# First loads on two queues, masks in another order, one sink product for all heads, and the spread of the inverse sums after the second turn

## The chip, the cores and the metric

The kernel runs on one core of a Trainium2 chip. The metric is the device time of one execution in microseconds (us). Three executions of the kernel before took 599.73, 600.29 and 600.51 us; their median, 600.29 us, is the time before.

## The reference

Attention over 2 batches of 8 heads, 768 positions and 64 dimensions, in which a position sees the last 128 positions (`window`) and the first 4 (`n_sink`), both given as run-time numbers. Then two feed-forward layers of 512 to 2048 to 512, each with weights in 64-bit floats, on the 1536 token rows.

```python
keep = is_sink | in_window                      # pos < n_sink, or 0 <= rel < window
scores = np.where(keep, scale * q @ k.T, -1e9)
a = np.exp(scores - max); a = a / (a.sum() + 1e-09)
x = (a @ v) as rows of 512
h = x @ w_in;  x = (h * tanh(log1p(exp(h)))) @ w_out        # first layer
h = x @ w_in2; x = (h * clip(h + 3, 0, 6) / 6) @ w_out2     # second layer
```

## The kernel before, in words

The token rows are cut into twelve units of 128 positions (all 8 heads each), numbered 0 to 11; units 0 to 5 are batch 0. `BLOCKS` groups them: 6, 7, 0, 1, then 2, 3, 4, 5, then 8 to 11. The eight units of the first two groups are done at the very start, in float32, by class `First` (lines 309 to 422); the last four are done later in pieces beside the layers. The layers split float32 values into two float16 parts and take three products for each.

For each of the eight first units, `prep` (L315) transposes keys and queries on TensorE (L323) and copies them out on ScalarE (L326); `scores(g)` (L337), for a half g of the heads, multiplies (L350), adds the mask and takes the minimum on VectorE (L354) and exponentiates on ScalarE (L358); `turn(g)` (L363) transposes the weights (L369) and copies them out (L371 on ScalarE, L373 on VectorE); `values(g)` (L382) multiplies by v (L393) into the PSUM tile `o`. Units at place 2 or later in their batch (units 2 to 5) see sink positions that lie outside their two blocks. For them `turn(g)` also gathers 16 sink columns for each of 4 heads (L377), transposes that (L379) and copies it out as `ats` (L380), and `values(g)` begins with two products of `ats` with `vsb` (L388), a block matrix of the first 16 value rows, built once on GpSimd (L306).

`inverse` (L398) takes the inverse of the sums on VectorE (L401, L402), spreads it over 64 columns on GpSimd (`rb`, L405), transposes that on TensorE (L407) and copies it out on ScalarE (`rib`, L409). `normalise` (L411) multiplies `o` by `rib` (`xf`, L413) and `outputs` (L415) splits the result (L419, L420).

`first_blocks` (L424) emits the steps of the eight units in an interleaved order: turn(0) of a unit, scores(0) of the next, outputs of the unit before, values(0), prep of the unit after the next, inverse, turn(1), scores(1) of the next, values(1), normalise. A scheduler then orders each engine's instructions: it keeps to the order of emission as priorities, and moves work that is ready into gaps. The decoding of the 64-bit weights on VectorE and ScalarE (L210 to L224) lies in such gaps. `keep_in_program_order` pins an instruction to its place.

At the start SP's queue issues, in this order, the two parameters (L110), keys and queries of the first unit (6), keys and queries of the second (7), then values, the third unit, and the first weights. VectorE sets three constants and zeroes `warm` (L929), on which 12 matmuls run (L932). `emit_params` (L107) turns the two parameters into floats as soon as they land, `emit_masks` (L122) builds the identity that all transposes use (`ident`, L128), the masks `m0`, `m1`, `m2` and the selector `selh`.

Of the kernel before, what the change touches and what calls it, by code (L numbers as in the profile page):

```python
# [7 lines left out]
F32 = mybir.dt.float32  # L8
# [21 lines left out]
def attention_moe_moe2(  # L30
# [59 lines left out]
    selh = const.tile([128, 4], F32)  # L90
    ident = const.tile([128, 128], F32)
# [15 lines left out]
    def emit_params():  # L107
        raw = const.tile([128, 2, 2], I32)
        for i, a in enumerate((n_sink, window)):
            nc.sync.dma_start(out=raw[:, i, :], in_=a.bitcast(I32).rearrange("(o t) -> o t", o=1).to_broadcast([128, 2]))  # L110
        f = const.tile([128, 2, 2], F32)
        t = const.tile([128, 2, 2], F32)
        nc.vector.tensor_copy(out=f, in_=raw)
# [8 lines left out]
    def emit_masks():  # L122
        ns, wd = nsw[:, 0:1], nsw[:, 1:2]
        tmp = part_p.tile([128, 4, 128], F32, tag="part", name="tmp")
        col, rel, ind, dg = (tmp[:, i] for i in range(4))
        nc.gpsimd.iota(col, pattern=[[1, 128]], base=0, channel_multiplier=0, allow_small_or_imprecise_dtypes=True)
        nc.gpsimd.iota(rel, pattern=[[-1, 128]], base=0, channel_multiplier=1, allow_small_or_imprecise_dtypes=True)
        nc.vector.tensor_scalar(out=ident, in0=rel, scalar1=0.0, scalar2=None, op0=ALU.is_equal)  # L128

        nc.vector.tensor_scalar(out=ind, in0=rel, scalar1=0.0, scalar2=None, op0=ALU.is_ge)  # L130
        nc.vector.scalar_tensor_tensor(out=dg, in0=rel, scalar=wd, in1=ind, op0=ALU.is_lt, op1=ALU.mult)
        nc.vector.tensor_scalar(out=m2[:, 0:128], in0=dg, scalar1=-BIG, scalar2=BIG, op0=ALU.mult, op1=ALU.add)

        nc.vector.scalar_tensor_tensor(out=ind, in0=col, scalar=ns, in1=dg, op0=ALU.is_lt, op1=ALU.max)
        nc.vector.tensor_scalar(out=m0, in0=ind, scalar1=-BIG, scalar2=BIG, op0=ALU.mult, op1=ALU.add)

        nc.vector.tensor_scalar(out=ind[:, 0:16], in0=col[:, 0:16], scalar1=ns, scalar2=None, op0=ALU.is_lt)
        nc.vector.tensor_scalar(out=m2[:, 256:272], in0=ind[:, 0:16], scalar1=-BIG, scalar2=BIG, op0=ALU.mult, op1=ALU.add)
# [6 lines left out]
        hp = const.tile([128, 4], F32)  # L145
        nc.gpsimd.iota(hp, pattern=[[-16, 4]], base=0, channel_multiplier=1, allow_small_or_imprecise_dtypes=True)
        a = const.tile([128, 4], F32)
        b_ = const.tile([128, 4], F32)
        nc.vector.tensor_scalar(out=a, in0=hp, scalar1=0.0, scalar2=None, op0=ALU.is_ge)
        nc.vector.scalar_tensor_tensor(out=a, in0=hp, scalar=16.0, in1=a, op0=ALU.is_lt, op1=ALU.mult)  # L150
        nc.vector.tensor_scalar(out=b_, in0=hp, scalar1=64.0, scalar2=None, op0=ALU.is_ge)
        nc.vector.scalar_tensor_tensor(out=b_, in0=hp, scalar=80.0, in1=b_, op0=ALU.is_lt, op1=ALU.mult)
        nc.vector.tensor_tensor(out=selh, in0=a, in1=b_, op=ALU.add)
# [133 lines left out]
    def load_first(u, names="kqv"):  # L287
        b, i = divmod(u, NSB)
        rows = slice(i * 128, (i + 1) * 128)
        for nm, src, pool, tag in (("k", k, n_p, "n"), ("q", q, n_p, "n"), ("v", v, v_p, "v")):  # L290
            if nm in names:
                t = pool.tile([128, H, D], F32, tag=tag, name="first")
                nc.sync.dma_start(out=t, in_=src[b, :, rows, :].rearrange("h p d -> p h d"))
                qkv_n.setdefault(u, {})[nm] = t

    def first_sinks(b):


        ks1 = c_p.tile([128, HP, 16], F32, name=f"ks1_{b}")
        nc.scalar.activation(out=ks1, in_=kv_n[b * NSB][0][:, :, 0:16], func=AF.Copy)  # L300
        vsn = c_p.tile([64, 2, D], F32, name=f"vsn_{b}")
        for g in range(2):
            nc.sync.dma_start(out=vsn[:, g, :], in_=v[b, 4 * g:4 * g + 4, 0:16, :])
        vsb = c_p.tile([64, 2, 4, D], F32, name=f"vsb_{b}")
        for h in range(4):
            nc.gpsimd.tensor_scalar(out=vsb[:, :, h, :], in0=vsn, scalar1=selh[0:64, h:h + 1], scalar2=None, op0=ALU.mult)  # L306
        sink_n[b] = (ks1, vsb)

    class First:
        def __init__(self, u):  # L310
            self.u = u
            self.b, self.i = divmod(u, NSB)
            self.d, self.at, self.ats = [None, None], [None, None], [None, None]
# [23 lines left out]
        def scores(self, g):  # L337
# [5 lines left out]
            for h0 in (4 * g, 4 * g + 2):  # L343
# [7 lines left out]
                for r in range(2):  # L351
                    h = h0 + r
                    hh = h % 4
                    nc.vector.tensor_tensor_reduce(  # L354
                        out=d[:, hh, 0:n], in0=sps[r], in1=self.mask, scale=SCALE, scalar=BIG,
                        op0=ALU.add, op1=ALU.min, accum_out=self.mins[:, h:h + 1],
                    )
                    nc.scalar.activation(  # L358
# [4 lines left out]
        def turn(self, g):  # L363
# [10 lines left out]
            if self.i > 1:  # L374
                ats = self.ats[g] = s_p.tile([64, 128], F32, tag="ats", name="ats")
                ds = s_p.tile([128, 4, 16], F32, tag="ds", name="ds")
                nc.vector.tensor_copy(out=ds, in_=d[:, :, 256:272])  # L377
                tp = ps_acc.tile([64, 128], F32, tag="acc", name="tp")
                nc.tensor.transpose(tp, ds.rearrange("p h s -> p (h s)"), ident)  # L379
                nc.vector.tensor_copy(out=ats, in_=tp)  # L380

        def values(self, g):  # L382
            if g == 0:
                self.o = ps_h.tile([128, HP, 128], F32, tag="h", name="o")
            if self.i > 1:
                for c in (2 * g, 2 * g + 1):
                    vsb = sink_n[self.b][1][:, g, 2 * (c % 2):2 * (c % 2) + 2].rearrange("p h d -> p (h d)")
                    nc.tensor.matmul(self.o[:, c, :], vsb, self.ats[g], start=c == 0, stop=False, skip_group_check=True)  # L388
            for c in (2 * g, 2 * g + 1):
                for m, kv in enumerate(self.kvs):  # L390
                    for r in range(2):
                        h = 2 * c + r
                        nc.tensor.matmul(  # L393
                            self.o[64 * r:64 * r + 64, c, :], kv[1][:, h, :], self.at[g][:, m, h % 4, :],
                            start=self.i <= 1 and c == 0 and m == 0, stop=c == HP - 1 and m == len(self.kvs) - 1, skip_group_check=True,
                        )

        def inverse(self):  # L398
# [3 lines left out]
            nc.vector.reciprocal(out=ri[:, :, 0], in_=rs)  # L402
            tp = ps_acc.tile([128, HP, 128], F32, tag="acc", name="tp")
            rb = b_p.tile([128, H, D], F32, tag="rb", name="rb")
            nc.gpsimd.tensor_copy(out=rb, in_=ri.to_broadcast([128, H, D]))  # L405
# [18 lines left out]
    def first_blocks():  # L424
# [4 lines left out]
        us[0].scores(0)  # L429
        us[1].prep(True)  # L430
        us[0].scores(1)
        for n, e in enumerate(us):
# [14 lines left out]
            e.turn(1)  # L447
            if f:
# [462 lines left out]

    nc.scalar.preload_act_table_set("natural_log_exp_and_others")
    nc.vector.memset(one, 1.0)
    nc.vector.memset(fifth, 0.2)
    nc.vector.memset(bias3, 3.0)
    emit_params()
    load_first(first[0], "kq")
# [69 lines left out]

    nc.vector.tensor_scalar(out=bads[:, 0:1], in0=nsw[:, 0:1], scalar1=16.0, scalar2=None, op0=ALU.is_gt)
    nc.vector.tensor_scalar(out=bads[:, 1:2], in0=nsw[:, 1:2], scalar1=128.0, scalar2=None, op0=ALU.is_gt)
    nc.vector.scalar_tensor_tensor(out=bads[:, 1:2], in0=nsw[:, 1:2], scalar=1.0, in1=bads[:, 1:2], op0=ALU.is_lt, op1=ALU.max)  # L990
# [190 lines left out]
NWARM = 12  # L1181
# [40 lines left out]
```

## Time and profile before

| what | value |
|---|---|
| three executions, median | 600.29 us (599.73 to 600.51) |
| the profiled execution, its own time | 599.53 us |
| its span, first to last instruction | 597.7 us |
| TensorE busy | 579.0 us, 97% of the span |
| VectorE busy | 457.8 us, 77% |
| ScalarE busy | 398.4 us, 67% |
| GpSimd busy | 24.8 us, 4% |

The profile is of one execution. Engines are called PE (TensorE matmul), PEld (TensorE weight load), DVE (VectorE), ACT (ScalarE), POOL (GpSimd) and SP (the sync engine, whose queue SPq issues loads). A row of the timeline has the start in us, the duration in us, engine, line, operation, output and inputs, a count where rows were merged, and in square brackets the idle time of the engine before it with what ended it. The chain of waits follows the execution back from its last instruction, at each step to what released it. About the first 97 us hold the eight first units; the layers fill the rest.

### The profile page before, as it was taken

To read this page: it belongs to the slowest core of one execution; us is meant where nothing else is said; L and a number is where in the kernel's file an instruction comes from. 1 tells how busy PE (TensorE), PEld (TensorE's weight loads), DVE (VectorE), ACT (ScalarE), POOL (GpSimd) and SP (SyncE) were. 2 spreads that over 40 slices of the span, in tenths; PEclk is the share of its full clock that TensorE was granted. 3 is DMA by queue.
4 is the path that set the end of the run, shared out by engine and by line. 5 is a ranking of instruction groups with operands and counts; after the bars stand their busy time and mean duration, and the time that the engine had idled before them with its cause. 6 is when DMAs were issued, how large, how long until landed. Compare 5 with 4: busy or idle time off the path is not lost.

```text
span 597.7 us, 11394 instructions
## 1 busy us (share of the span) xinstructions
PE 579.0 (97%) x4430; PEld 394.4 (66%) x4430; DVE 457.8 (77%) x1102; ACT 398.4 (67%) x786; POOL 24.8 (4%) x36
## 2 busy tenths in 40 slices
PE   7999999999999999899989999999999999999996
PEld 4778754444444545444434468888888888888885
DVE  5688998999365555489999999866687889874754
ACT  5998887777687776679888887434354656553532
POOL 0040010700000000000000000000000000000000
PEclk9999999999999999999999999999999999999999
DMA  9976357998334533254453442000007676400001
GB/s 179 226 163 212 101 183 199 230 261 213 96 73 74 80 60 73 47 159 141 157 192 122 163 143 71 1 1 2 1 7 249 215 263 223 142 34 1 36 1 39
DMA packets 105842, 72.24 MB, mean 121 GB/s; under 512 B 73512, under 2 KB 98088, under 8 KB 105784
## 3 DMA queue, kind: packets, MB, share of 16 engines
q1 hardware_dynamic: 105784, 71.48, 42.9%
q8 instruction: 35, 0.57, 0.4%
q14 instruction: 23, 0.19, 0.1%
HBM read 60.43 MB, written 3.15 MB: 106 GB/s over the span
## 4 chain that ended last, share of the span: by engine, by line
PE 59%; DVE 13%; ACT 12%; issue 11%; DMA 2%; POOL 2%; SPq 1%; DVEq 0%; ACTq 0%
PE acc L846 18%; PE h L806 7%; PE h L808 7%; PE h L807 7%; PE acc L782 6%; PE h L737 3%; PE h L739 2%; PE h L738 2%; DVE p L212 2%; ACT e L745 2%; ACT e L746 2%; DVE g L754 2%; ACT d L358 2%; ACT y L215 1%; PE o L393 1%
## 5 line engine op out<-in xcount | busy, mean ns | idle before, releaser
L782 PE MATMUL acc<-g,w 128*128 128x512 f16 x576 | 131.2, 379 | 5.4 <-DVE g L754 5.1
L846 PE MATMUL acc<-w,g 128*128 128x256 f16 x1008 | 113.8, 273 | 0.0
L846 PEld LDWEIGHTS <-g 128*128 128x128 f16 x1008 | 98.6, 98 | 11.4
L806 PE MATMUL h<-xt,w 128*128 128x256 f16 x384 | 104.7, 273 | 0.0
L808 PE MATMUL h<-xt,w 128*128 128x256 f16 x384 | 104.7, 273 | 0.0
L807 PE MATMUL h<-xt,w 128*128 128x256 f16 x384 | 104.7, 273 | 0.0
L782 PEld LDWEIGHTS <-w 128*128 128x128 f16 x576 | 55.3, 98 | 71.6 <-issue 7.0
L737 PE MATMUL h<-xt,w 128*128 128x512 f16 x192 | 72.8, 379 | 1.8 <-DVE mins L558 1.2
L739 PE MATMUL h<-xt,w 128*128 128x512 f16 x192 | 72.8, 379 | 0.0
L738 PE MATMUL h<-xt,w 128*128 128x512 f16 x192 | 72.8, 379 | 0.0
L810 ACT ACTIVATE e<-h,bias 128x512 f32<-128x512 f32 x48 | 32.5, 678 | 54.5 <-PE h L808 54.5
L811 DVE SCALAR_TENSOR_TENSOR e<-e,h 128x512 f32<-128x512 f32 x48 | 32.8, 684 | 41.8 <-ACT e L810 41.8
L823 ACT ACTIVATE g<-e 128x256 f16<-128x256 f32 x96 | 29.5, 354 | 28.8 <-DVE e L811 28.8
L823 ACT ACTIVATE g<-sm 128x512 f16<-128x512 f32 x48 | 30.2, 628 | 27.5 <-DVE sm L818 27.5
L749 DVE SCALAR_TENSOR_TENSOR e<-e,h 128x512 f32<-128x512 f32 x48 | 30.8, 683 | 16.5 <-ACT e L747 16.3
L824 DVE SCALAR_TENSOR_TENSOR g<-sm,g 128x512 f16<-128x512 f32 x48 | 33.1, 689 | 10.9 <-ACT g L823 10.8
L806 PEld LDWEIGHTS <-w 128*128 128x128 f16 x384 | 37.6, 98 | 4.6
L807 PEld LDWEIGHTS <-w 128*128 128x128 f16 x384 | 37.6, 98 | 4.5
L808 PEld LDWEIGHTS <-w 128*128 128x128 f16 x384 | 37.6, 98 | 4.3
L212 DVE SCALAR_TENSOR_TENSOR p<-raw,y 128x1024 int32<-128x1024 int32 x32 | 39.8, 1243 | 0.4
L740 ACT ACTIVATE e<-h 128x512 f32<-128x512 f32 x48 | 28.1, 588 | 16.4 <-PE h L739 16.4
L754 DVE SCALAR_TENSOR_TENSOR g<-e,g 128x1024 f16<-128x1024 f32 x24 | 29.4, 1226 | 8.3 <-ACT g L753 8.3
(172 smaller groups left out, 934.8 us busy)
## 6 DMA issues: line engine op xcount, KB each, us to landing
raw<-in_moe_w_in_dram SPq DMA_DIRECT2D x48, 512.0 KB, 4.2
raw<-in_moe_w_out_dram SPq DMA_DIRECT2D x48, 512.0 KB, 5.0
out_dram<-ob SPq DMA_DIRECT2D x12, 256.0 KB, 2.5
first<-in_k_dram SPq DMA_DIRECT2D x8, 256.0 KB, 4.8
first<-in_q_dram SPq DMA_DIRECT2D x8, 256.0 KB, 4.9
first<-in_v_dram SPq DMA_DIRECT2D x8, 256.0 KB, 3.1
nk<-in_k_dram SPq DMA_DIRECT2D x5, 256.0 KB, 5.1
nv<-in_v_dram SPq DMA_DIRECT2D x5, 256.0 KB
```

What stands on the lines that cost most here:

```text
L212: nc.vector.scalar_tensor_tensor(out=p, in0=t[:, :, 1], scalar=3, in1=y, op0=ALU.logical_shift_left, op1=ALU.bitwise_xor)
L737: nc.tensor.matmul(o, wh, x[:, 0, c, :], start=c == 0, stop=False)
L738: nc.tensor.matmul(o, wh, x[:, 1, c, :], start=False, stop=False)
L739: nc.tensor.matmul(o, wl, x[:, 0, c, :], start=False, stop=c == KD - 1)
L754: nc.vector.scalar_tensor_tensor(out=gl, in0=e, scalar=sc, in1=gh, op0=ALU.mult, op1=ALU.subtract)
L782: nc.tensor.matmul(o, l_, r_, start=first and m == 0 and x == 0, stop=last and end and x == 2, skip_group_check=True)
L806: nc.tensor.matmul(o, wh, x[:, 0, c, :], start=c == 0, stop=False)
L807: nc.tensor.matmul(o, wh, x[:, 1, c, :], start=False, stop=False)
L808: nc.tensor.matmul(o, wl, x[:, 0, c, :], start=False, stop=c == KD - 1)
L823: nc.scalar.activation(out=g[:, 0, d_], in_=src, func=AF.Copy, scale=sc)
L824: nc.vector.scalar_tensor_tensor(out=g[:, 1, d_], in0=src, scalar=sc, in1=g[:, 0, d_], op0=ALU.mult, op1=ALU.subtract)
L846: nc.tensor.matmul(a[n // 2][:, n % 2], l_, r_, start=f == fa and m == 0 and n % 2 == 0 and x == 0, stop=ends and m == 1 and x == 2 and (n ...
```

## The change

It has these parts. At the start the parameters' loads are issued first, the first unit's keys go on ACT's queue and its queries on SP's; only then does ACT load its function table. On DVE `warm` is zeroed ahead of the three constants; `emit_fixed` builds `ident`, the causal indicator and the selectors before the parameters are converted; `emit_masks` builds only `m0`; the other masks and three range flags (`bads`, formerly emitted at the end) follow scores(0) of the first unit. Most of these are pinned to their order. There are 10 warm matmuls in place of 12.

For the sinks, `ds` gathers all 8 heads, one transpose and one copy of `ats` make 128 rows in place of 64 twice, `vsb` covers 128 rows with 8 GpSimd instructions in place of 4, its load is one DMA in place of two, and the sink products stand at the end of `values(1)` and no longer ahead of each half.

`inverse` keeps its DVE and POOL part; the four transposes of `rb` and the copy of `rib` move into `spread`, which is emitted after turn(1).

```diff
+    raw_p = load_params()
+    load_first(first[0], "k", nc.scalar)
+    load_first(first[0], "q")
     nc.scalar.preload_act_table_set("natural_log_exp_and_others")
-    emit_params()
-    load_first(first[0], "kq")
     load_first(first[1], "kq")
...
     nc.vector.memset(warm, 0.0)
+    nc.vector.memset(one, 1.0)
+    nc.vector.memset(fifth, 0.2)
+    nc.vector.memset(bias3, 3.0)
+    fixed = emit_fixed()
+    emit_params(raw_p)
...
-    emit_masks()
+    emit_masks(fixed)
...
-        us[0].scores(0)
+        us[0].scores(0, True)
+        emit_later_masks(fixed)
         us[1].prep(True)
...
             e.inverse()
             e.turn(1)
+            e.spread()
...
             if self.i > 1:
-                ats = self.ats[g] = s_p.tile([64, 128], F32, tag="ats", name="ats")
-                ds = s_p.tile([128, 4, 16], F32, tag="ds", name="ds")
-                nc.vector.tensor_copy(out=ds, in_=d[:, :, 256:272])
-                tp = ps_acc.tile([64, 128], F32, tag="acc", name="tp")
-                nc.tensor.transpose(tp, ds.rearrange("p h s -> p (h s)"), ident)
-                nc.vector.tensor_copy(out=ats, in_=tp)
+                if g == 0:
+                    self.ds = b_p.tile([128, H, 16], F32, tag="ds", name="ds")
+                nc.vector.tensor_copy(out=self.ds[:, 4 * g:4 * g + 4, :], in_=d[:, :, 256:272])
+                if g == 1:
+                    self.ats = b_p.tile([128, 128], F32, tag="ats", name="ats")
+                    tp = ps_acc.tile([128, 128], F32, tag="acc", name="tp")
+                    nc.tensor.transpose(tp, self.ds.rearrange("p h s -> p (h s)"), ident)
+                    nc.vector.tensor_copy(out=self.ats, in_=tp)
...
-            if self.i > 1:
-                for c in (2 * g, 2 * g + 1):
-                    vsb = sink_n[self.b][1][:, g, 2 * (c % 2):2 * (c % 2) + 2].rearrange("p h d -> p (h d)")
-                    nc.tensor.matmul(self.o[:, c, :], vsb, self.ats[g], start=c == 0, stop=False, skip_group_check=True)
...
+            if self.i > 1 and g == 1:
+                for c in range(HP):
+                    vsb = sink_n[self.b][1][:, 2 * c:2 * c + 2].rearrange("p h d -> p (h d)")
+                    nc.tensor.matmul(self.o[:, c, :], vsb, self.ats, start=False, stop=c == HP - 1, skip_group_check=True)
...
-NWARM = 12
+NWARM = 10
```

## Rows read from the trace of the kernel before

**Rows 1.** Busy us by stretch: length, PE, PEld, DVE, ACT, POOL, PEclk, DMA share, GB/s

```profile
9.00:20.00 11.00, 9.88 (x98) 7.88 (x100) 5.97 (x36) 10.92 (x41) 1.09 (x3) 1.00 1.24 259
20.00:30.00 10.00, 9.33 (x97) 7.07 (x94) 7.72 (x35) 8.89 (x29) 0.99 (x2) 1.00 0.75 192
...
40.00:50.00 10.00, 9.54 (x96) 7.99 (x97) 7.18 (x24) 8.88 (x25) 1.12 (x3) 1.00 0.59 190
...
60.00:72.00 12.00, 11.40 (x112) 9.33 (x112) 11.77 (x37) 9.89 (x28) 0.81 (x2) 1.00 0.28 89
72.00:97.00 25.00, 25.00 (x162) 13.93 (x162) 23.68 (x37) 19.71 (x29) 1.57 (x1) 1.00 0.63 191
97.00:150.00 53.00, 51.45 (x257) 23.18 (x256) 48.38 (x72) 40.52 (x57) 11.53 (x11) 1.00 0.89 226
```

**Rows 2.** Timeline of the first 10 us, all engines

```profile
0.80 1.28 ACT L912 ACT_TABLE_LOAD   x1 [0.80 <-PEq L1202]
...
1.35 4.30 PE L932 MATMUL wp<-warm 128*128 128x512 f16 x12 [1.35 <-DVE ones L998]
...
1.75 0.43 SPq L293 DMA_DIRECT2D first<-in_k_dram  x1
...
2.23 0.58 SPq L293 DMA_DIRECT2D first<-in_q_dram  x1
...
4.31 0.17 DVE L113 CAST f<-raw 128x4 f32<-128x4 int32 x1 [3.01 <-DMA raw<-in_window_dram]
...
6.34 1.09 PE L323 MATMUL tp<-ident,first 128*128 128x128 f32 x8 [0.69 <-DVE ident L128]
...
7.52 0.59 ACT L326 ACTIVATE qt<-tp 128x512 f32<-128x512 f32 x1
...
8.56 0.23 DVE L143 TENSOR_SCALAR m_all<-tmp 128x128 f32<-128x128 f32 x1
...
8.74 0.29 DVE L354 CUSTOM_DVE_ANT_0 d<-s,m 128x128 f32<-128x128 f32 x1
...
9.08 0.40 ACT L358 ACTIVATE d<-d,mins 128x128 f32<-128x128 f32 x1 [0.96 <-DVE mins L354]
```

**Rows 3.** DMA issues between 2.0 and 2.5 us: last number, us to landing

```profile
first<-in_q_dram SPq DMA_DIRECT2D x1, 256.0 KB, 4.4
```

**Rows 4.** Chain of waits, 15 to 88 us: start, us on the chain, what

```profile
15.23 0.44 PE tp L407 x4
...
24.43 0.60 PE tp L407 x4
...
59.14 1.07 POOL rb L405
60.25 0.67 PE tp L407 x4
60.94 0.60 ACT rib L409
...
87.40 0.59 PE tp L407 x4
```

**Rows 5.** Timeline of ACT, DVE, POOL and PE at `rib`, `xf` and the sinks

```profile
16.68 0.59 ACT L409 ACTIVATE rib<-tp 128x512 f32<-128x512 f32 x1
...
18.94 0.69 DVE L413 TENSOR_TENSOR xf<-o,rib 128x512 f32<-128x512 f32 x1 [0.49 <-PE o L393]
...
31.39 3.98 POOL L306 TENSOR_SCALAR vsb<-vsn,selh 64x128 f32<-64x128 f32 x4
...
46.24 0.71 PE L388 MATMUL o<-ats,vsb 64*128 64x128 f32 x4
...
49.57 0.60 ACT L409 ACTIVATE rib<-tp 128x512 f32<-128x512 f32 x1
...
54.07 0.69 DVE L413 TENSOR_TENSOR xf<-o,rib 128x512 f32<-128x512 f32 x1
```

**Rows 6.** Groups by line and shape up to 95 us: busy us, mean ns, idle before

```profile
L380 DVE COPY ats<-tp 64x128 f32<-64x128 f32 x8 | 2.2, 275 | 1.0 <-PE tp L379 1.0
```

More of the change, by code (lines that the diff above doesn't have):

```diff
@@ L90, in attention_moe_moe2 @@
     selh = const.tile([128, 4], F32)
+    sel8 = const.tile([128, H], F32)
     ident = const.tile([128, 128], F32)
@@ L120, in emit_params, with emit_fixed @@
         nc.vector.tensor_tensor(out=nsw, in0=t[:, :, 0], in1=t[:, :, 1], op=ALU.mult)
-    def emit_masks():
+    def emit_fixed():
+        tmp = part_p.tile([128, 4, 128], F32, tag="part", name="tmp")
+        col, rel, ind = (tmp[:, i] for i in range(3))
+        hp = const.tile([128, 4], F32)
+        nc.gpsimd.iota(rel, pattern=[[-1, 128]], base=0, channel_multiplier=1, allow_small_or_imprecise_dtypes=True)
+        nc.gpsimd.iota(col, pattern=[[1, 128]], base=0, channel_multiplier=0, allow_small_or_imprecise_dtypes=True)
+        nc.gpsimd.iota(hp, pattern=[[-16, 4]], base=0, channel_multiplier=1, allow_small_or_imprecise_dtypes=True)
+        keep_order(nc.vector.tensor_scalar(out=ident, in0=rel, scalar1=0.0, scalar2=None, op0=ALU.is_equal))
+        keep_order(nc.vector.tensor_scalar(out=ind, in0=rel, scalar1=0.0, scalar2=None, op0=ALU.is_ge))
+        a, b_ = (sel8[:, 0:4], sel8[:, 4:8])
+        keep_order(nc.vector.tensor_scalar(out=a, in0=hp, scalar1=0.0, scalar2=None, op0=ALU.is_ge))
+        keep_order(nc.vector.tensor_scalar(out=b_, in0=hp, scalar1=64.0, scalar2=None, op0=ALU.is_ge))
+        keep_order(nc.vector.scalar_tensor_tensor(out=a, in0=hp, scalar=16.0, in1=a, op0=ALU.is_lt, op1=ALU.mult))
+        keep_order(nc.vector.scalar_tensor_tensor(out=b_, in0=hp, scalar=80.0, in1=b_, op0=ALU.is_lt, op1=ALU.mult))
+        keep_order(nc.vector.tensor_tensor(out=selh, in0=a, in1=b_, op=ALU.add))
+        return tmp
@@ L123, in emit_masks @@
+    def emit_masks(tmp):
         ns, wd = nsw[:, 0:1], nsw[:, 1:2]
-        tmp = part_p.tile([128, 4, 128], F32, tag="part", name="tmp")
         col, rel, ind, dg = (tmp[:, i] for i in range(4))
-        nc.gpsimd.iota(col, pattern=[[1, 128]], base=0, channel_multiplier=0, allow_small_or_imprecise_dtypes=True)
-        nc.gpsimd.iota(rel, pattern=[[-1, 128]], base=0, channel_multiplier=1, allow_small_or_imprecise_dtypes=True)
-        nc.vector.tensor_scalar(out=ident, in0=rel, scalar1=0.0, scalar2=None, op0=ALU.is_equal)
@@ L140, in emit_masks, with emit_later_masks @@
+    def emit_later_masks(tmp):
+        ns, wd = nsw[:, 0:1], nsw[:, 1:2]
+        col, rel, ind, dg = (tmp[:, i] for i in range(4))
+        keep_order(nc.vector.tensor_scalar(out=m2[:, 0:128], in0=dg, scalar1=-BIG, scalar2=BIG, op0=ALU.mult, op1=ALU.add))
         nc.vector.tensor_scalar(out=dg, in0=rel, scalar1=128.0, scalar2=wd, op0=ALU.add, op1=ALU.is_lt)
@@ L292, in load_first @@
                 t = pool.tile([128, H, D], F32, tag=tag, name="first")
-                nc.sync.dma_start(out=t, in_=src[b, :, rows, :].rearrange("h p d -> p h d"))
+                ld = eng.dma_start(out=t, in_=src[b, :, rows, :].rearrange("h p d -> p h d"))
+                if pin:
+                    keep_order(ld)
                 qkv_n.setdefault(u, {})[nm] = t
@@ L300, in first_sinks @@
         nc.scalar.activation(out=ks1, in_=kv_n[b * NSB][0][:, :, 0:16], func=AF.Copy)
[L301 to L306, printed above, removed]
+        vsn = c_p.tile([128, D], F32, name=f"vsn_{b}")
+        nc.sync.dma_start(out=vsn, in_=v[b, :, 0:16, :])
+        vsb = c_p.tile([128, H, D], F32, name=f"vsb_{b}")
+        for h in range(H):
+            nc.gpsimd.tensor_scalar(out=vsb[:, h, :], in0=vsn, scalar1=sel8[:, h:h + 1], scalar2=None, op0=ALU.mult)
         sink_n[b] = (ks1, vsb)
@@ L312, in __init__ @@
             self.b, self.i = divmod(u, NSB)
-            self.d, self.at, self.ats = [None, None], [None, None], [None, None]
+            self.d, self.at = [None, None], [None, None]
         def prep(self, pin=False):
@@ L335, in prep, with scores @@
             self.mask = (m0, m1, m2)[min(i, 2)]
-        def scores(self, g):
+        def scores(self, g, pin=False):
             n = self.n
@@ L357, in scores @@
                     )
+                    if pin:
+                        keep_order(low)
                     nc.scalar.activation(
@@ L402, in inverse, with spread @@
             nc.vector.reciprocal(out=ri[:, :, 0], in_=rs)
+            self.rb = rb = b_p.tile([128, H, D], F32, tag="rb", name="rb")
+            nc.gpsimd.tensor_copy(out=rb, in_=ri.to_broadcast([128, H, D]))
+        def spread(self):
+            rb = self.rb
             tp = ps_acc.tile([128, HP, 128], F32, tag="acc", name="tp")
-            rb = b_p.tile([128, H, D], F32, tag="rb", name="rb")
-            nc.gpsimd.tensor_copy(out=rb, in_=ri.to_broadcast([128, H, D]))
             for c in range(HP):
```

44 lines of the change are left out of this document (17 added, 27 removed).

## The prediction

> **What bounds the kernel now.** I read the stretches first, then the timeline of the start, then the chain of waits. From 72 us on PE has work in nearly every microsecond: it is busy 25.00 of 25 us up to 97 and 51.45 of 53 up to 150 [rows 1]. Nothing in the change touches the layers, so what it can win lies in the first 97 us and shows as an earlier start of the layers. Those 97 us have several limits. Up to 9.08 us, when the first exponential runs, everyone waits for the start [rows 2]. From 9 to 20 us ACT is the limit, 10.92 busy of 11. From 20 to 30 and from 40 to 50 no engine is full: PE has 9.33 and 9.54 of 10, but its instructions overlap and that is latency, not work; DVE has 7.72 and 7.18, so 2.3 and 2.8 us in which DVE stands in the middle of a dependent chain. From 60 us on DVE is all but full: 11.77 of 12, 23.68 of 25, 48.38 of 53, because the decoding of weights fills its gaps [rows 1]. A shorter chain helps in full only where no engine is full.
>
> A measurement of this kernel can tell a difference of about 0.2%, 1.2 us, from no change; below 599.1 us counts as faster, above 601.5 as slower.
>
> **The start.** The queries are issued at 2.23 us and land 4.4 us later, at 6.63 [rows 2, 3]. The transposes stand at 6.34, after 0.69 us in which PE waited for `ident`, which is built behind the parameters although it doesn't need them; then come the copy of the queries at 7.52, the first mask operation at 8.74 and the exponential at 9.08. Two things arrive together at 8.74: the scores, and DVE itself, which builds `m1` until 8.79 (L143) before it turns to the scores [rows 2].
>
> Moving the keys to ACT's queue lets the queries take the SP place of the keys, 1.75 us, 0.48 us earlier. If the earlier keys (ACT is free at 0.80, some 0.9 us before 1.75) merely start the same stream of bytes earlier, the queries land 0.9 us earlier; if the second queue brings nothing, 0.48. With `ident` done before any key lands, the key transposes and their copy lie ahead of the queries, and the copy of the queries starts at landing + 0.55 (half of 1.09 for 8 transposes) + 0.1, so 7.28 by today's landing against 7.52: 0.24 us. Together 0.7 to 1.1 us. DVE's side keeps up: the parameters are converted at 4.31, seven operations of about that row's 0.17 us end at 5.5, and three mask operations, each as long as L143 (0.23) or half as long again, end `m0` near 6.5, where 7.7 is wanted; that is a cover of 1.2 us if the parameters land as now [rows 2]. The removed warm matmuls (2 of 12 in 4.30 us, 0.4 to 0.7 us of filler) lie in the 0.69 us PE idles before its first transpose: cost nothing. If PE ran its first transposes and scores at half rate for want of them, 1.09 us would double; that end I keep for the range. The later masks and range flags, ten DVE operations at the 0.23 us of L143, 2.3 us, move behind the first scores, where DVE waits for PE anyway; if they come in front of scores(1) they cost up to 0.5. The load that ACT now issues itself (0.43 us, as the same load takes on SP) pushes its table load of 1.28 us from 0.80 to 1.3; its first copy, of the keys, comes after 5 us [rows 2]. I take 1.0 us; ends 0 and 1.4. ACT is full from 9 to 20, so this shift is carried on whole as long as the loads keep ahead.
>
> The row that prices the second queue is the 4.4 us of one load among others [rows 3]; no row here has a load on ACT's queue. The Trainium skill, page "DMA: Bandwidth & Descriptors", section "Issuing engines are not separate DMA queues", says that loads started by different engines run on the same 16 DMA engines and interleave, so that only issue time is saved. By it the keys also stand in the way of the parameters; the start would win about 0.5 us, and the sum would be 2.7 in place of 3.2. The DMA share of 1.24 from 9 to 20 us [rows 1] agrees as far as it goes: the engines are the limit there, not the issuer.
>
> **The spread of the inverse sums.** Today PE has to run the four transposes of `rb` before the second turn, though turn(1) needs only exponentials that are done when POOL starts. At 59 us this is plain: POOL's 1.07 us, PE's 0.67 and ACT's 0.60 lie on the chain one behind the other. Ten such pieces, from 15.23 to 87.40 us, all others of 0.44 to 0.62, make 6.1 us [rows 4]. They are not removed, they go behind turn(1) and its copies, which the values wait for. At 15 and 87 us a full engine lies beside them, about 1.0 us that wins nothing. Of the 5.1 left, those at 24, 41 and 49 us (2.1 us) lie where DVE idles and count almost whole; those from 59 us on lie where DVE has under 1 us to spare [rows 1]. What is late next is the copy of the weights on ACT and the mask operations behind decoding. I take 1.6 us; ends 0 (another order of waits) and 5.1. `rib` itself comes about 1 to 1.5 us later. In the first unit it is done at 17.27 and wanted at 18.94, room of 1.7 us; in the fifth 50.17 and 54.07, room of 3.9 [rows 5].
>
> **The sinks.** Four units have them. For each, one of two transposes goes and one of two copies of `ats` on DVE (8 rows of 275 ns, some 0.2 us each where they overlap with the next [rows 6]). The products keep their count, four passes of 128 columns in 0.71 us for each half [rows 5]; on 128 rows they stream the same 128 columns, and I leave them at their price (ends: none, or a third of 8 x 0.71 = 5.7 us less). The first products no longer stand ahead of the values of half 0. DVE's 4 x 0.2 = 0.8 us counts, since DVE is full there; PE's transposes lie beside it. I take 0.6; ends 0 and 2.0. GpSimd's `vsb` becomes eight operations over half the columns: between 4 and 8 us in place of 3.98. It is built by 35.4 us and first read at 46.24, so 11 us hide it [rows 5]; at the upper end the next `rb` on POOL could be late by 2 us. One load fewer on SP, 0.6 us, hides too.
>
> **The sum.** 1.0 + 1.6 + 0.6 = 3.2 us. The profiled execution took 599.53 us (span 597.7 and 1.8 around it); 3.2 less is 596.3. The median lies 0.76 higher, so 597.1.
>
> **Rivals.** *DVE holds it.* From 60 to 150 us DVE is 91 to 98% busy, and what leaves the chain is refilled by the same decoding; PE then waits for DVE after 97 us, where today it idles only 1.55 us of 53 [rows 1]. Only DVE's own saving and part of the start come through: 0.8 + 0.4 = 1.2, so 599.3 (about no change). For it: those rows. Against: before 50 us DVE idles over 5 us in the two open stretches, and the decoding can be done earlier when everything is earlier. Chance 0.18.
>
> *Only issue time is saved at the start*, by the mechanism above: the keys and the queries share the 16 engines, and the tiny parameter loads share with them, so that `m0` comes as late as the scores. The start gives 0.5: 597.6. Chance 0.13, and faster all the same.
>
> *All that left the chain counts:* 1.2 + 4.0 + 1.3 = 6.5, so 593.8. The chain of waits lists these pieces one behind the other, which is for it; DVE's fill from 60 us is against. Chance 0.13.
>
> *`rib` becomes the last input of `xf`.* ACT copies it after the weights and, if the next unit's exponentials get in between (four of 0.40 us or longer [rows 2]), about 3 us later than now. Rooms are 1.7 to 3.9 us; the point from which it decides is about 2 us of delay. `xf` then holds the PSUM tile `o`, from the pool that the next scores use, and each of four units would lose 1.4 us (3.1 less 1.7): 5.6 lost, 2.6 won (start, spread partly, sinks), 3.0 slower: 603.3. Against it: `spread` is emitted ahead of scores(1) of the next unit, so its priority is higher. Chance 0.08.
>
> **Numbers.** My forecast has 0.48. Faster: 0.48 less a small tail of its own (0.02 to no change), and 0.13 and 0.13: 0.72. No change: 0.18 and that tail: 0.20. Slower: 0.08. The likeliest case gives 597.1, by itself 595 to 599. The range reaches down to 593.8, where all counts, and up to 600.3, where all three terms are at their lower ends: 593.8 to 600.3.
>
> **What would show it.** Right: the first exponential near 8.0 us in place of 9.08; first transposes no longer released by `ident` but by a load; no wait of PE for `rb`, and turn(1) ahead of the transposes of `rb` in every unit; four copies of `ats` in place of eight; PE full from about 69 us, where the layers' matmuls now begin at 72; and PE as full as before from 97 us on. Wrong: the first exponential later than 8.6 (parameters or queries landed late); `xf` waiting for ACT instead of PE; or an early first layer matmul followed by new waits of PE for DVE between 97 and 180 us, which would give the win back.

## The result: slower by 6 us, and the profile after

The changed kernel takes 606.09 us (median of 4 runs, 603.94 to 608.11), the kernel before 600.02 (median of 4 runs on the same chip); the ratio is 1.0103 with a 95% interval of 1.0085 to 1.0122. The forecast was 597.1, the range ended at 600.3: wrong in sign. The execution profiled took 603.94 us (span 602.1), so its trace explains 4.4 of the 6 us. Line numbers move with the change: L210, L211, L212 and L224, the four DVE steps of a weight decoding, are L224, L225, L226 and L238 now; L749 and L754, the layer's own DVE steps, which write `e` and `g`, are L773 and L778.

First the stretches of the changed kernel, columns as in [rows 1]:

```profile
9.00:20.00 11.00, 9.54 (x93) 7.37 (x93) 7.01 (x41) 10.58 (x41) 1.09 (x3) 1.00 1.18 254
...
72.00:97.00 25.00, 24.82 (x172) 14.60 (x169) 24.07 (x43) 20.01 (x31) 1.50 (x1) 1.00 0.60 187
97.00:150.00 53.00, 49.09 (x244) 21.84 (x243) 48.32 (x72) 40.21 (x57) 11.64 (x11) 1.00 0.92 239
```

The layers are hit, whose code the change doesn't touch: between 97 and 150 us PE is busy 49.09 of 53 us where it had 51.45, while DVE does what it did (48.32 against 48.38). The first layer matmul comes at 73.62 us, 1.2 later than before (72.41), and the 168th of the matmuls into `acc` (L782, now L806) at 165.58, 4.5 later (161.07): 3.3 us are lost in between. Now the start, from the timeline of all engines:

```profile
0.80 0.45 ACTq L307 DMA_DIRECT2D first<-in_k_dram  x1
...
1.25 0.23 DVE L136 TENSOR_SCALAR ident<-tmp 128x128 f32<-128x128 f32 x1
...
5.22 0.17 DVE L120 CAST f<-raw 128x4 f32<-128x4 int32 x1 [3.07 <-DMA raw<-in_window_dram]
...
5.50 1.65 PE L338 MATMUL tp<-ident,first 128*128 128x128 f32 x8
...
8.47 0.29 DVE L369 CUSTOM_DVE_ANT_0 d<-s,m 128x128 f32<-128x128 f32 x1 [1.03 <-PE s L365]
...
8.81 0.40 ACT L375 ACTIVATE d<-d,mins 128x128 f32<-128x128 f32 x1 [1.01 <-DVE mins L369]
...
12.30 0.41 PE L338 MATMUL tp<-ident,first 128*128 128x128 f32 x2 [1.38 <-DMA first<-in_k_dram]
```

The first exponential stands at 8.81 in place of 9.08 [rows 2]: 0.27 us won of the 1.0 forecast. The parameters land 0.9 us later than before (5.22 against 4.31), since the keys are now in front of them. And at 12.3 us PE waits 1.38 us for the third unit's keys: two of their transposes now stand ahead of the second unit's scores, which start at 12.64 where they started at 11.74. So the scheduler, not the source, turned the start into a loss.

The second place is the end of the first layer's decoding. Here are DVE and ACT's part of `e` in the kernel before, from its timeline:

```profile
139.07 0.76 DVE L210 TENSOR_SCALAR y<-raw 128x1024 int16<-128x1024 int16 x1 [0.66 <-DMA raw<-in_moe_w_out_dram]
139.72 0.74 DVE L211 TENSOR_SCALAR y<-raw 128x1024 int16<-128x1024 int16 x1
...
140.15 1.04 ACT L747 ACTIVATE e<-e 128x1024 f32<-128x1024 f32 x1
...
141.22 1.28 DVE L749 SCALAR_TENSOR_TENSOR e<-e,h 128x512 f32<-128x512 f32 x2 [0.76 <-ACT e L747]
142.42 1.22 DVE L224 SCALAR_TENSOR_TENSOR w<-p,w 128x1024 f16<-128x1024 f32 x1
...
144.69 1.22 DVE L754 SCALAR_TENSOR_TENSOR g<-e,g 128x1024 f16<-128x1024 f32 x1
```

and in the changed kernel, with two waits of PE for DVE:

```profile
132.61 0.38 PE L761 MATMUL h<-xt,w 128*128 128x512 f16 x1 [1.54 <-DVE e L773]
...
142.47 1.22 DVE L226 SCALAR_TENSOR_TENSOR p<-raw,y 128x1024 int32<-128x1024 int32 x1
...
143.78 1.04 ACT L771 ACTIVATE e<-e 128x1024 f32<-128x1024 f32 x1
...
144.32 0.76 DVE L224 TENSOR_SCALAR y<-raw 128x1024 int16<-128x1024 int16 x1 [0.64 <-DMA raw<-in_moe_w_out_dram]
144.97 0.76 DVE L225 TENSOR_SCALAR y<-raw 128x1024 int16<-128x1024 int16 x1
145.60 1.28 DVE L773 SCALAR_TENSOR_TENSOR e<-e,h 128x512 f32<-128x512 f32 x2
...
149.19 1.23 DVE L778 SCALAR_TENSOR_TENSOR g<-e,g 128x1024 f16<-128x1024 f32 x1
...
150.47 2.75 PE L806 MATMUL acc<-g,w 128*128 128x512 f16 x12 [1.38 <-DVE g L778]
```

It is the same work in another order: before, `e` stands behind the first two steps of the 16th decoding; now the fourth step of the 15th, the third of the 16th and two steps of the 17th, the first of these waiting for its load, stand ahead of it as well. `e` comes 4.4 us later, `g` 4.5, but most of that was lost earlier: ACT's part of `e` ends 3.6 us later already (144.82 against 141.19). Before, `e` starts 0.03 us behind that end, now 0.78, with DVE busy on decode steps in between; so this place itself accounts for 0.8 us. PE's larger wait, 1.54 us at 132.61, has no counterpart in the kernel before; the `e` that it waits for starts at 131.88, only 0.4 behind the end of ACT's part, so this trace doesn't say what made most of that wait.

### The profile page after: what moved, and what is told of

The parts are those of the page before. It is cut to its first block, busy times and chain, and to the rows that moved or that the text cites. A ratio compares the mean times of both kernels' runs of the same rounds, so it can differ in the third digit from the quotient of the medians.

```text
span 602.1 us, 11391 instructions
## 1 busy us (share of the span) xinstructions
PE 579.9 (96%) x4424; PEld 395.6 (66%) x4424; DVE 458.5 (76%) x1098; ACT 398.4 (66%) x786; POOL 25.8 (4%) x40
## 4 chain that ended last, share of the span: by engine, by line
PE 59%; DVE 13%; issue 11%; ACT 11%; DMA 3%; POOL 2%; SPq 2%; ACTq 0%; DVEq 0%; POOLq 0%
PE acc L870 18%; PE h L831 7%; PE h L832 7%; PE h L830 7%; PE acc L806 6%; PE h L761 3%; PE h L763 2%; PE h L762 2%; DVE p L226 2%; ACT e L769 2%; ACT e L770 2%; PE s L365 2%; DMA nk<-in_k_dram 1%; ACT y L229 1%; DVE g L778 1%
## 5 line engine op out<-in xcount | busy, mean ns | idle before, releaser
L806 PE MATMUL acc<-g,w 128*128 128x512 f16 x576 | 131.2, 379 | 6.6 <-DVE g L778 5.5
L806 PEld LDWEIGHTS <-w 128*128 128x128 f16 x576 | 55.4, 98 | 72.9 <-issue 8.7
L773 DVE SCALAR_TENSOR_TENSOR e<-e,h 128x512 f32<-128x512 f32 x48 | 30.8, 681 | 19.0 <-ACT e L771 18.8
L226 DVE SCALAR_TENSOR_TENSOR p<-raw,y 128x1024 int32<-128x1024 int32 x32 | 39.7, 1242 | 0.5
L778 DVE SCALAR_TENSOR_TENSOR g<-e,g 128x1024 f16<-128x1024 f32 x24 | 29.3, 1220 | 8.4 <-ACT g L777 8.3
```

Of the source, the lines that this page charges most:

```text
L226: nc.vector.scalar_tensor_tensor(out=p, in0=t[:, :, 1], scalar=3, in1=y, op0=ALU.logical_shift_left, op1=ALU.bitwise_xor)
L778: nc.vector.scalar_tensor_tensor(out=gl, in0=e, scalar=sc, in1=gh, op0=ALU.mult, op1=ALU.subtract)
L806: nc.tensor.matmul(o, l_, r_, start=first and m == 0 and x == 0, stop=last and end and x == 2, skip_group_check=True)
```

## The experiments

All times are medians, beside runs of the kernel before on the same chip (599.87 to 599.97). The theories, as the first expectations name them: **A**, the new start carries the loss by its loads and their order; **B**, the later spread carries it; **C**, any change of the first 72 us shifts the decoding on DVE. From the second set on C is sharpened to **D**: DVE's order behind 72 us carries it. **E** (the loads of weights come later) and **F** (PE's clock) are its rivals.

**One part at a time.** Three kernels each make one part of the change on the kernel before, a fourth the sinks and the spread together: the changed kernel less its start.

The start alone (the keys' queue, the masks' order, 10 warm matmuls):

```diff
+    load_first(first[0], "k", nc.scalar)
+    load_first(first[0], "q")
...
+    fixed = emit_fixed()
+    emit_params(raw_p)
...
-        us[0].scores(0)
+        us[0].scores(0, True)
+        emit_later_masks(fixed)
```

> Only the start of the change (keys on ACT's queue, order of constants, masks and flags, 10 warm matmuls); sinks and spread as before. Theory A, the start carries the loss: PE's order puts two transposes of the third unit's keys ahead of the second unit's scores, PE waits about 1.4 us there for a load, as in the changed kernel at 12.3 us, and the layers' first matmul comes at 73 us or later; 603 to 606 us. Theory B, the later spread carries the loss: this kernel has the gain of the start alone, first exponential near 8.8 us, 599 to 600 us.

Measured: 607.12 us, ratio 1.0102 [1.0070, 1.0134].

The later spread alone:

```diff
             e.turn(1)
+            e.spread()
```

> Only the later spread of the inverse sums; start and sinks as before. Theory A: no load wait of PE at 12 us, the pieces that left the chain come through in part, 598 to 600 us. Theory B: PE waits for rb in at least four units, 1.5 to 2 us in all up to 72 us, and the layers start later than 72.4 us; 602 to 605 us. Theory C, any new order of DVE's work shifts the decoding, and what is lost is lost after 97 us: PE waits over 2 us for DVE between 97 and 165 us whatever the part, 601 to 604 us.

Measured: 600.50 us, 1.0011 [1.0002, 1.0021].

The sinks alone (`first_sinks`, and the sinks' parts of `turn` and `values`):

```diff
+        vsn = c_p.tile([128, D], F32, name=f"vsn_{b}")
+        nc.sync.dma_start(out=vsn, in_=v[b, :, 0:16, :])
...
+                    nc.tensor.matmul(self.o[:, c, :], vsb, self.ats, start=False, stop=c == HP - 1, skip_group_check=True)
```

> Only the sinks of all heads at once; start and spread as before. Theories A and B: eight passes take 1.0 us a unit in place of 1.28 and four copies fall away, 598.5 to 600 us. Theory C: PE waits over 2 us for DVE between 97 and 165 us here too, 601 to 604 us.

Measured: 600.52 us, 1.0007 [0.9997, 1.0016]. No theory has these numbers whole: the start costs more than A's range, and the other two lie between A's and C's.

Sinks and spread together:

> Sinks and later spread, with the start as before. Theory A: 597 to 599.5 us, faster than before. Theory B: 601 to 605 us. Theory C: 601 to 604 us with the loss after 97 us.

Measured: 604.50 us, 1.0065 [1.0039, 1.0090]. Parts that cost 0.6 us each cost 4.6 together; no sum of costs does that, so B falls, and A can't be all. In the traces the later spread alone is 0.9 us ahead of the kernel before at the 32nd of the matmuls into `acc` (L782; 101.92 against 102.81), and 1.1 behind at the 168th (162.20 against 161.07): won early, lost in the layers. With both parts, DVE's timeline shows how, and PE's what follows:

```profile
143.79 0.75 DVE L210 TENSOR_SCALAR y<-raw 128x1024 int16<-128x1024 int16 x1 [2.16 <-DMA raw<-in_moe_w_out_dram]
144.44 1.27 DVE L754 SCALAR_TENSOR_TENSOR e<-e,h 128x512 f32<-128x512 f32 x2
...
146.91 0.38 PE L787 MATMUL acc<-g,w 128*128 128x512 f16 x1 [1.38 <-ACT g L758]
...
149.31 6.81 PE L787 MATMUL acc<-g,w 128*128 128x512 f16 x23 [2.02 <-DVE g L759]
```

DVE waits 2.16 us for a load with `e` behind it; PE waits 1.38 and 2.02; and then 23 matmuls take 6.81 us that take 5.12 in other places. That is the clock: behind the waits PE drops to the lower level, 1.2 GHz. Stretches of this kernel:

```profile
146.00:149.80 3.80, 0.87 (x4) 0.35 (x4) 3.80 (x6) 3.77 (x6) 0.00 (x0) 1.00 0.57 130
149.90:153.20 3.30, 3.30 (x9) 1.18 (x8) 2.07 (x4) 2.35 (x3) 0.00 (x0) 0.50 1.04 213
153.40:160.00 6.60, 6.60 (x32) 3.00 (x31) 1.46 (x2) 1.65 (x2) 0.00 (x0) 1.00 0.00 1
```

**The orders swapped.** If D holds, the order alone must make and mend the loss. In these kernels the decodings' four steps and `e` and `g` are queued on DVE, from the first layer on, in the order of the *other* kernel; the edges add no wait between engines. They hold DVE alone: the scheduler orders the other engines anew around it.

```diff
+    seen = {c: iter(x) for c, x in steps_by.items()}
+    line = [next(seen[c]) for c in DVE_ORDER]
+    for x, y in list(zip(line, line[1:]))[DVE_FROM:]:
+        tc.add_manual_dep(
+            y.ins, x.ins.name,
...
+        )
```

`steps_by` collects the instructions as they are emitted, and `DVE_ORDER` is the order as a string (1 to 4 the decoding's steps, `e`, `g`). Its end is `...g23412ee3g142312ee4g3142eegeeg` in the kernel before and `...34123ee4g123124312ee4geegeeg` in the changed one. The changed kernel with the order of the kernel before:

> The changed kernel, with one thing taken from the kernel before: from the first layer on, the 16 weight decodings' four DVE steps and the layer's own DVE steps (e, g) stand on DVE in the order in which they stand in the kernel before. Theory D (the loss behind 72 us is DVE's order: a decode step that still waits for its load, or one decode tile too many, stands ahead of e): the trace loses only what it has lost by the first layer matmul (1.2 us), so 600.5 to 602; e of the eighth step at 142 to 143 us and not at 145.6; no wait of PE for DVE over 1.3 us between 100 and 155. Rival E (the weights land later because other loads were moved, the order only shows it): 604 to 607, DVE waits 2 us and more for a load at the same places. Rival F (PE's clock carries it): as E, with half-rate stretches behind 97 us.

Measured: 601.46 us, 1.0024 [1.0014, 1.0034]; 4.6 us come back. The one trace of this kernel is of its slowest execution (604.62 us of 600.28 to 604.62), with a drop of PE's clock at 12.30 us, so it doesn't show where. It agrees with D in part: PE's order is that of the changed kernel, PE waits 1.20 us for DVE at most between 100 and 155 us, and `e` starts 0.03 us behind ACT's part,

```profile
146.03 1.28 DVE L782 SCALAR_TENSOR_TENSOR e<-e,h 128x512 f32<-128x512 f32 x2 [0.94 <-ACT e L780]
```

but `e` was expected at 142 to 143, the trace loses 2.3 us more behind its first layer matmul (74.93 us), and DVE waits 2.22 us for a load of weights at 118.95, as E has it, though at another place. The kernel before with the order of the changed one:

> The kernel before, with the changed kernel's order of the decode steps and of e and g on DVE from the first layer on; nothing else of the change. Theory D: slower by 3 to 5 us, 603 to 605, lost between 97 and 165 us, e of the eighth step 3 to 4 us later than 141.2. Rivals E and F: 599 to 601, since no load and no start is touched.

Measured: 602.20 us, 1.0041 [1.0026, 1.0056], 2.3 us lost, a little less than expected, with no load and no start touched; its trace is at 72.42 us with the first layer matmul (72.41 before) and 2.4 us late at the 168th into `acc` (163.51 against 161.07). ACT's part of `e`, DVE and PE there:

```profile
140.66 1.04 ACT L756 ACTIVATE e<-e 128x1024 f32<-128x1024 f32 x1
...
144.99 0.74 DVE L215 TENSOR_SCALAR y<-raw 128x1024 int16<-128x1024 int16 x1
145.61 0.74 DVE L216 TENSOR_SCALAR y<-raw 128x1024 int16<-128x1024 int16 x1
146.23 1.28 DVE L758 SCALAR_TENSOR_TENSOR e<-e,h 128x512 f32<-128x512 f32 x2
...
146.97 0.38 PE L746 MATMUL h<-xt,w 128*128 128x512 f16 x1 [1.35 <-DVE e L758]
```

ACT's part is done at 141.70, and `e` starts 4.53 us later, 5.0 us later than in the kernel before, behind other work on DVE that waits for no load there. E and F fall as causes in this kernel: the weights are issued in the same order, DVE waits for one of them 0.96 us at most (1.01 in the kernel before), and the granted clock of this execution was 1.000. A few other instructions have another place too (nine of PE's matmuls, eight of them near 145 us, three transfers on SP, a dozen steps on ACT); no run holds these as well. In other kernels the clock comes on top: the profiled executions of the start alone (608.15 us) and of both parts (604.40) have such a drop, the fastest of the same kernels took 603.55 and 601.74.

Two kernels take the start's own misplacement away: the third unit's key transposes are pinned behind the first unit's values,

```diff
-                us[n + 2].prep()
+                us[n + 2].prep(n == 0)
```

with the changed kernel's order on DVE, and with that of the kernel before:

> The changed kernel with the third unit's key transposes pinned behind the first unit's values on PE, so that the second unit's scores no longer stand behind a load that lands at 12.3 us. If that order is what the start loses: scores of the second unit at 11.6 to 11.8 us in place of 12.64, first layer matmul near 72.6 in place of 73.61. Theory D says the total stays at 603 to 606 all the same, because DVE's order from the first layer on is nearly that of the changed kernel. If the start alone carries the loss: 599 to 600.5.

Measured: 603.95 us, 1.0067 [1.0045, 1.0088]. The total is as D says, but the first layer matmul came at 74.41, not near 72.6: what the pin won at the start (fourth normalisation 44.40 against 45.05) was gone by the fifth (55.71 against 55.20).

> Both: the pin of the third unit's key transposes and the order of the kernel before on DVE from the first layer on. Theory D and the start's order together: what is left is the win of the spread and the sinks in the first 72 us, 0 to 1.5 us: 598.5 to 600.3. Rivals E and F: 603 to 606.

Measured: 601.14 us, 1.0026 [1.0006, 1.0046]: 2.8 us better by the late order, but above what was expected. Its trace is 2.0 us late at 103 us already, lost between 44 and 56 us, where the order on DVE had been left free.

**The whole order held.** First the pair that had lost 4.6 us, and the spread alone, with the old order from the layers on:

> The kernel before with the sinks and the later spread (604.5 us without more), and with the kernel before's order of the decode steps and of e and g on DVE from the first layer on. Theory D (DVE's order behind 72 us): the 4 to 5 us come back whole, 599.0 to 600.2; no half-rate stretch of PE near 150 us, no wait of PE for g over 1.3 us there. Rival (the sinks and the spread cost by their own work or by the clock): 602.5 to 605.

Measured: 600.52 us, 1.0007 [0.9997, 1.0017]; 4.0 us come back, a little less than expected, no execution of ten lies above 601.02, and nothing is won.

> The kernel before with the later spread alone (600.5 us without more), and the kernel before's order on DVE from the first layer on. Its trace was 0.9 us ahead of the kernel before at 103 us and lost 2.0 by 161 us. Theory D: the 2.0 come back, 598.8 to 599.6, the first win of any version. Rival (what the spread wins is refilled by DVE in any order): 599.7 to 600.6.

Measured: 600.11 us, 1.0002 [0.9991, 1.0014]. The total is the rival's, and no win is shown. In the trace the lead of 0.8 us is kept at 188 us, as D says, and is 0.1 from 302 us on: at 297.71 DVE waits 0.82 us for a load of weights with `e` behind it, and PE then waits 0.64 us for `g` where it waits 0.15 in the kernel before. Then the changed kernel with the pin and, from the first unit on, the order of the later-spread version also among mask operations and normalisations:

> The changed kernel with the third unit's key transposes pinned, and on DVE, from the end of the first unit on, the whole order of the kernel with the later spread alone up to the layers (decode steps among mask operations and normalisations), and that of the kernel before behind it. The version with only the second of these two orders (601.1) still came 2.0 us late to 103 us, lost between 44 and 56 us with one more decoding ahead of the fifth unit's normalisation. If that too is DVE's order: 598.0 to 599.8, the fifth normalisation at 52.5 to 53.5 us in place of 55.9. If the new start loses it in another way: 600.5 to 602.

Measured: 599.28 us, 0.9998 [0.9989, 1.0007]. The fifth normalisation stands at 52.59 and the trace is 1.55 us ahead at 103 us, so the loss before the layers hung on DVE's order too. Yet the lead was gone by 113 us, in an instruction that the list didn't hold. DVE's timeline of this version:

```profile
100.47 1.23 DVE L231 SCALAR_TENSOR_TENSOR p<-raw,y 128x1024 int32<-128x1024 int32 x1
103.87 0.29 DVE L642 SCALAR_TENSOR_TENSOR vsl<-vsn,vsh 128x128 f16<-128x128 f32 x1 [2.17 <-ACT vsh L641]
105.81 0.94 DVE L229 TENSOR_SCALAR y<-raw 128x1024 int16<-128x1024 int16 x1 [1.65 <-DMA raw<-in_moe_w_out_dram]
```

An operation of 0.29 us held DVE for 2.17. With the five kinds of splits for the second batch in the list as well:

> The last version (599.3 us) once more, and the other splits on DVE behind 72 us (keys, values, queries and the sinks' values of the second batch) in the order of the later-spread version too. In the last version's trace the win of 1.55 us at 103 us was lost by 113: the sinks' split of values stood ahead of a decode step and waited 2.17 us, and the weights were issued behind those values on SP. If that was the whole loss: 1.2 to 1.6 us ahead of the kernel before at 161 us, 598.0 to 598.9 in all, below the kernel before by more than a measurement is uncertain. If what is won early is refilled anyway: 599.2 to 600.2.

Measured: 597.99 us (597.52 to 598.60), ratio 0.9967 [0.9954, 0.9979]. This is the changed kernel's work in a good order, and it beats both: 8.1 us below the changed kernel, 2.0 below the kernel before. Its trace, of the slowest of six executions, is 1.1 us ahead at 103 us and 0.8 at 161, less than the expected 1.2 to 1.6. No run puts this list on the kernel before, so how much of the 2.0 is the change's own and how much the list's isn't shown. Its start and the place at 140 us, from the timelines of ACT, PE and DVE:

```profile
8.53 0.40 ACT L385 ACTIVATE d<-d,mins 128x128 f32<-128x128 f32 x1 [1.00 <-DVE mins L378]
...
11.18 1.16 PE L374 MATMUL s<-kt,qt 64*128 64x128 f32 x16 [0.55 <-ACT qt L350]
...
140.41 1.28 DVE L783 SCALAR_TENSOR_TENSOR e<-e,h 128x512 f32<-128x512 f32 x2 [1.52 <-ACT e L781]
...
143.88 1.22 DVE L788 SCALAR_TENSOR_TENSOR g<-e,g 128x1024 f16<-128x1024 f32 x1
```

Here DVE waits for ACT's part of `e`, and not `e` for DVE; `g` stands 5.3 us ahead of the changed kernel's. Without the pin, all else alike:

> The same without the pin: the third unit's first two key transposes stand ahead of the second unit's scores on PE again. If that order costs on the path of the start: second unit's scores at 12.4 to 12.7 us and not at 11.6 to 11.8, 0.8 to 1.2 us more than with the pin (599.0 to 600.0), with now and then a half-rate stretch of PE behind its wait. If it is hidden: the same as with the pin within 0.3.

Measured: 601.17 us, 1.0024 [1.0013, 1.0035]: 3.2 us without the pin, far more than the 1.4 us by which the second unit's scores are late. From the timelines of PE, ACT and DVE:

```profile
12.21 0.41 PE L347 MATMUL tp<-ident,first 128*128 128x128 f32 x2 [1.52 <-DMA first<-in_k_dram]
12.55 1.16 PE L374 MATMUL s<-kt,qt 64*128 64x128 f32 x16
...
32.35 1.05 ACT L244 ACTIVATE w<-p 128x1024 f16<-128x1024 f32 x1
...
33.43 1.27 DVE L246 SCALAR_TENSOR_TENSOR w<-p,w 128x1024 f16<-128x1024 f32 x1 [3.50 <-ACT w L244]
```

and ACT with the pin:

```profile
25.16 1.06 ACT L244 ACTIVATE w<-p 128x1024 f16<-128x1024 f32 x1
```

Its third normalisation is 4.2 us later than with the pin (37.39 against 33.23), and ahead of it a decode step keeps DVE waiting 3.50 us for ACT (L246): the copy that this step needs (L244) has another place on ACT, whose order is free, and starts 7.2 us later. The list holds DVE alone, and another engine's order shifted under it. How much of the 3.2 is the transposes' own isn't told apart.

**The second queue by itself.** The kernel before with the keys on ACT's queue, nothing else of the start, and its own order on DVE:

```diff
+    load_first(first[0], "k", nc.scalar)
     nc.scalar.preload_act_table_set("natural_log_exp_and_others")
...
-    load_first(first[0], "kq")
+    load_first(first[0], "q")
```

> The kernel before with one edit of the start alone: the first unit's keys are issued from ACT's queue; masks, identity and warm matmuls stay, and DVE keeps the kernel before's order from the end of the first unit on. The parameters land 0.9 us later behind the keys and here the identity hangs on them: transposes 0.6 to 0.9 us later, the first exponential at 9.3 to 9.6 in place of 9.08, 600.0 to 601.0 in all. If the second queue by itself makes the start faster: first exponential at 8.2 to 8.7, 599.0 to 599.7.

Measured: 607.11 us, 1.0114 [1.0099, 1.0129]. The start behaves as expected in kind, and 0.3 us worse in size:

```profile
5.15 0.17 DVE L113 CAST f<-raw 128x4 f32<-128x4 int32 x1 [3.84 <-DMA raw<-in_window_dram]
...
7.17 1.09 PE L332 MATMUL tp<-ident,first 128*128 128x128 f32 x8 [0.51 <-DVE ident L128]
...
9.91 0.40 ACT L368 ACTIVATE d<-d,mins 128x128 f32<-128x128 f32 x1 [0.96 <-DVE mins L363]
```

The parameters are late by 0.8 us and `ident` behind them, so the first exponential is 0.83 late. The total missed by 6 us, and most of that lies behind the start: the first normalisation is 1.2 us late, the fifth 2.2, the sixth 5.8 (70.97 against 65.13). Twice DVE waits 2.20 us for the sink transpose that it copies to `ats` (53.05 and 64.12), and this copy is not in the list; in the kernel before the same copies wait 0.80 us and not at all. DVE is then full from 66 to 71.5 us, PE waits for the normalisation, and from 71.6 us on runs at the lower level. What the queue alone is worth in the total isn't shown. From PE's timeline and the stretches:

```profile
71.80 0.55 PE L359 MATMUL s<-kt,qt 64*128 64x128 f32 x1 [2.49 <-DVE xf L423]
...
66.00:71.50 5.50, 3.31 (x39) 2.73 (x37) 5.46 (x13) 3.00 (x8) 0.00 (x0) 1.00 0.49 150
71.60:78.30 6.70, 6.50 (x41) 5.75 (x42) 3.83 (x17) 3.66 (x12) 0.93 (x1) 0.50 0.08 30
```

## Why the prediction was wrong

**The step that failed** is the one under all three terms: that what leaves the first 72 us shows as an earlier start of the layers, and that nothing behind 72 us changes because "nothing in the change touches the layers". Of the 4.4 us in the changed kernel's trace 1.2 were lost ahead of the layers and 3.3 in them. The order on each engine is the scheduler's. It moves work that it takes to be ready into gaps, and each of the three edits moved those gaps. In the kernel before with nothing but the changed kernel's order on DVE, decode steps hold `e` for 4.53 us, PE waits behind it, and 2.3 us are lost. In others they stand ahead of their loads as well: DVE waits for weights 2.25 us at most with sinks and spread together and 4.24 with the start alone, where the kernel before has 1.01; in the changed kernel itself the longest is 1.75. The prediction named the sign of this ("an early first layer matmul followed by new waits of PE for DVE between 97 and 180 us"), and its rival *DVE holds it* has such waits, but only as a win that is used up: 1.2 us faster, which is 599.1 and not the 599.3 given there. That a new order could cost more than the change wins had no rival, no price and no chance; nor was the start early, as that sign supposed. Against *DVE holds it* it argued that decoding "can be done earlier when everything is earlier". It can't be earlier than its load, and it took the place of work that others waited for. The rival on the slower side was the wrong one: `rib` was not the input that `xf` waited for. In the changed kernel `xf` still waits for PE.

**The start, 1.0 us.** Mis-sized, then undone. The first exponential came later than the 8.6 us that the prediction had named as a sign of being wrong. How far the first exponential moves depends on when PE's clock comes up, so compare kernels where it reaches the full level at about the same time: at 5.38 us the old start gives 9.03 and at 5.47 the new one 8.54; at 6.69 and 6.76 it is 9.26 and 8.81; at 6.01 and 6.11, 9.13 and 8.53. That is 0.45 to 0.60 us: the 0.48 of the issue slot and little more. The queries still land 4.4 us after their issue, and the parameters land 0.8 to 1.0 us later. The rival *only issue time is saved*, with its chance of 0.13, was right on this term. The Trainium skill, page "DMA: Bandwidth & Descriptors", section "Issuing engines are not separate DMA queues", says that loads issued by different engines interleave on the same DMA engines and that only the issuing time is saved. The trace agrees, with the 0.45 to 0.60 us. The cover of 1.2 us for `m0` shrank to 1.0 (done at 7.45, wanted at 8.47) and held. The later masks cost ACT nothing: its exponentials run on without a gap from 8.81 to 12.9 us. The end "PE at half rate" for the first transposes came true (1.65 us for 8 against 1.09), but kernels with 12 warm matmuls reach the full level anywhere from 4.10 to 6.72 us as well, so the two that were removed aren't shown to be the cause. Two keys' transposes ahead of the scores then took 0.9 us, more than all of this.

**The later spread, 1.6 us.** Right in kind, smaller in size, and nothing of it in the total: alone it is ahead by 1.37 us at the second normalisation (26.56 against 27.93) and 0.9 at 103 us, and measures 600.50 us, or 600.11 with the order held. The sign "no wait of PE for `rb`" did not come: in the changed kernel it waits for it four times, 1.7 us in all, 0.7 at most. `rib` was late for nothing.

**The sinks, 0.6 us.** The work went as forecast and nothing came of it: the eight passes take 1.16 us for a unit,

```profile
54.01 1.16 PE L415 MATMUL o<-ats,vsb 128*128 128x128 f32 x8
```

in place of two times 0.71 [rows 5], a term that had been left at its price, and yet alone the part was 0.9 us late at 103 us and measures as no change.

**The sum.** With the order held and one misplaced step pinned, change and list together win 2.0 us (1.3 to 2.8 by the interval of the ratio) of the 3.2 forecast. What the change sets off in the scheduler cost four times as much: 8.1 us lie between two orders of the same work.

## What to carry to other kernels

Where a scheduler fills gaps, an edit that makes the front of a kernel earlier re-deals every in-order queue behind it: before a forecast, list the instructions that could stand ahead of the critical step on a full engine, those that wait for a load first, and give "the order comes out worse" its own chance and price. When parts that measure zero alone cost microseconds together, compare the order of the fullest engine first, and test it by putting one kernel's order on the other, both ways. Once it is shown, pin the few steps that wait for loads. A list for one engine holds that engine alone: the others are ordered anew around it, and an instruction that the list leaves out can still slip in ahead and wait.

## What the runs showed of the hardware

PE's clock fell to the lower level in the middle of the kernel, and PE had not stood still long: with sinks and spread together it had worked 0.87 of the 3.80 us before, its longest wait 2.02, and was then granted 0.50 for 3.4 us; in the kernel with the start alone the waits were 1.75 and 2.02 us, the clock fell during the second, and the lower level held for 6.8. A wait for DVE can thus be paid twice, but isn't always: single waits of PE of 2.60 us (the changed kernel with pin and whole order, at 112.87) and 1.91 (sinks and spread with the old order, at 112.83) passed without a drop. The traces of the kernel before and of the best version show no drop until the end. One more stands at 12.30 us in the profiled execution of the changed kernel with the old order, right behind PE's wait for the keys; there the first normalisation comes at 20.65 us, 1.3 later than in the changed kernel's own trace.

How soon the full level first comes is not fixed by the kernel: between 4.10 and 7.10 us over these traces, with the same 12 warm matmuls from 4.10 to 6.72.
